# Four sigmoids and a tanh in place of exp, log1p and squared sums in a fused attention and feed-forward kernel

## The chip, the cores and the metric

The kernel runs on one core of a Trainium2 chip. The metric is the device time of one execution in microseconds (us). A core has engines that run side by side[...]: TensorE (PE in the profile, with PEld for its weight loads), VectorE (DVE), ScalarE (ACT), GpSimd (POOL) and SyncE (SP), which here only issues DMAs.

## The reference

Hashed attention comes first: queries and keys are hashed to six bits, and a query sees only the keys of its bucket. There are 4 x 8 heads of 768 x 64. Its output, as 3072 tokens of 512 values, goes through a feed-forward block:

```python
def _moe_ref(x, w_in, w_out) -> np.ndarray:   # x 3072x512, w_in 512x2048, w_out 2048x512
    h = x @ w_in
    sp = np.maximum(h, 0.0) + np.log1p(np.exp(-np.abs(h)))
    g = h * erf(sp)
    return (g @ w_out).astype(np.float32)
```

The activation is thus h times erf(log(1 + exp(h))). The change concerns only how erf(log(1 + exp(h))) is computed.

## The kernel before

The program has two stages. The attention stage takes some 320 us; it makes x and, beside its matmuls, brings the weights into SBUF. Its instructions are the same in both kernels. Then `feed_forward` runs, with everything in fp32.

`feed_forward` takes the tokens in 6 tiles of 512, and each tile in 4 chunks of the 2048 hidden values, so there are 24 chunks, numbered p. In each chunk both matrix products are done by a Strassen scheme of seven half-size products:

- `product` (L1204) makes P1 to P7, the parts of h, with four matmuls of 128x256 each. They go into one PSUM bank X, in the order P1, P6, P7, P4, P2, P5, P3, each after the bank has been emptied. `read` (L1222, ACT) copies a part from the bank into h in SBUF, `complete` (L1226, DVE) adds a later part to it. In the first three chunks, while the output banks are not in use, the products use those instead of X.
- The elementwise work runs on two units of a chunk, v = 0 and 1, of 128x1024 elements each: 48 units in all. A unit is ready when its four parts have been read and completed.
- `presum_g` (L1301, DVE) makes the sums of the activated h that Strassen's scheme wants, and `project` (L1344) makes M1 to M7 with four matmuls each, summed in PSUM over the four chunks of a tile. `combine` (L1359 on ACT, L1375 on DVE) puts the seven sums of a tile together and sends the output.

One unit passes through these steps before the change:

| step | engine, line | what it does |
|---|---|---|
| clip | DVE L1233 | e = min(h, 3.98) |
| exponential | ACT L1239 | e = exp(e) |
| one_more | ACT L1243 | w = 1 + e |
| lost | DVE L1248 | w = (w - 1) - e, the rounding lost in 1 + e |
| logarithm | ACT L1254 | e = log(1 + e) |
| correct | DVE L1258 | s = e - w |
| square | ACT L1262 | z = s squared |
| factor, 3 times | ACT L1267 | q = (z + c) squared, c from the tile cq |
| multiply, 3 times | DVE L1271 | s = (q + constant) * s |
| saturate | ACT L1282 | s = tanh(constant * s) |
| gate | DVE L1286 | h = h * s |

exp and log lie in different activation tables, so table loads (ACT_TABLE_LOAD) stand between them in ACT's queue.

The order of the instructions on every engine is fixed when the program is built, by `arrange` (L118). It is a list scheduler: each step is given as an `Op` with an engine, a cost, what it comes after, and a rank. The products and reads have ranks that begin with 0, the elementwise steps and `project` with 1 and then p plus a due time from `PRIORITY`. At each step the planner takes, on each engine, the ready step that can start first, and by rank where several can; it adds 1.28 where an ACT step changes the table. It also counts buffers:

```python
for each in arrange(ops, dict(h=8, e=4, w=6, wt=2), PATIENCE):
    each.emit()
```

There are eight tiles h (two per chunk), four tiles e, six tiles w, and two tiles wt for weight sums, which SP reloads from DRAM. The engines then work through their fixed orders, each waiting where its next instruction isn't ready.

Of the kernel before, what the change touches and what calls it, by code (L numbers as in the profile page):

```python
# [54 lines left out]
F32 = mybir.dt.float32  # L55
# [3 lines left out]
AF = mybir.ActivationFunctionType  # L59
ALU = mybir.AluOpType  # L60
# [3 lines left out]
P = 128  # L64
# [3 lines left out]
TINY = 3.242492675781250e-05  # L68
EPS = 2.0**-100
BOUND = 40.0  # L70
H_MAX = 3.98
ERF_LEAD = 1.418517747371711e-07
ERF_Q = (
    (6.2794604751645355, 19.35174303303216),
    (-5.316226701641483, 239.37499811839012),
    (-20.943483610527835, 66.98472325796595),
)


# [1 line left out]
class Op:  # L81
# [16 lines left out]


PRIORITY = dict(  # L100
    clip=(-0.37, 0.71),
    exponential=(3.56, 5.29),
    one_more=(4.45, -12.01),
    lost=(-10.26, -0.21),
    logarithm=(-0.61, 0.06),
    correct=(-8.09, -7.53),
    square=(-0.08, -1.35),
    factor=((-5.24, -2.71, -0.94), (-0.59, 2.14, 1.15)),
    multiply=((-3.33, 5.43, 8.37), (-6.26, 8.92, -4.28)),
    saturate=(-9.79, -1.73),  # L110
    gate=(9.64, -1.5),
    presum_g=(4.49, -4.94, 6.75, 0.67),
    project=-7.76,
)
# [79 lines left out]
def kernel(  # L194
# [11 lines left out]
    nc = tc.nc  # L206
# [16 lines left out]
    scale = 1.0 / D**0.5  # L223
    assert D == 64 and S == 768 and DM == JP * P and NT == B * S and NK == 4

    const = ctx.enter_context(tc.tile_pool(name="const", bufs=1))
# [10 lines left out]
    ones = const.tile([P, D], F32, name="ones")  # L237
    sgn = const.tile([P, 1], F32, name="sgn")
    tiny2 = const.tile([P, 1], F32, name="tiny2")
    cq = const.tile([P, len(ERF_Q)], F32, name="cq")  # L240
    w_in_sb = const.tile([P, NK, DFF], F32, name="w_in_sb")
    w_out_sb = const.tile([P, NF, DM], F32, name="w_out_sb")
    w_sum = const.tile([P, 3, 2, FH], F32, name="w_sum")
# [7 lines left out]
    for ab in range(2):  # L251
        rows = slice(ab * D, ab * D + D)
        nc.vector.tensor_copy(
            out=proj_sb[rows, ab * QR : ab * QR + NBIT],
            in_=proj_in[rows, ab * NBIT : (ab + 1) * NBIT],
# [4 lines left out]
    for c, (end, factor) in enumerate(  # L260
# [12 lines left out]
            out=steps[:, c : c + 1],  # L273
            in0=row,
            scalar1=float(end),
            scalar2=factor * BIG,
            op0=ALU.is_lt,
            op1=ALU.mult,
# [4 lines left out]
    for ab in range(2):  # L283
        rows = slice(ab * D, ab * D + D)
        nc.vector.tensor_copy(
            out=proj_q[rows, ab * QB : ab * QB + NBIT],
            in_=proj_in[rows, ab * NBIT : (ab + 1) * NBIT],
# [3 lines left out]
    nc.vector.tensor_copy(out=weight_q[D + QR : P, :], in_=weight_q[D : D + QR, :])  # L291
    nc.vector.memset(sgn, -(2.0**-27))
    nc.vector.memset(tiny2, TINY * TINY)
    for j, (c, _) in enumerate(ERF_Q):
        nc.vector.memset(cq[:, j : j + 1], c)

    def bank(name):
# [859 lines left out]
    def feed_forward(check, late):  # L1157
        again = late is None
        with (
# [11 lines left out]
            st = {}  # L1171

            def own(what):
                return work.tile([P, 2 * T], F32, name=what, tag=what, bufs=dict(e=4, w=6)[what])
# [53 lines left out]
            def unit(p, v):  # L1228
                return st[p]["h", v][:, :, :, :].rearrange("p f u t -> p (f u t)")

            def clip(p, v):
                e = st[p]["e", v] = own("e")
                nc.vector.tensor_scalar(  # L1233
                    out=e, in0=unit(p, v), scalar1=H_MAX, scalar2=None, op0=ALU.min
                )

            def exponential(p, v):
                e = st[p]["e", v]
                nc.scalar.activation(out=e, in_=e, func=AF.Exp)  # L1239

            def one_more(p, v):
                w = st[p]["w", v] = own("w")
                nc.scalar.activation(out=w, in_=st[p]["e", v], func=AF.Identity, bias=1.0)  # L1243

            def lost(p, v):

                w = st[p]["w", v]
                nc.vector.scalar_tensor_tensor(  # L1248
                    out=w, in0=w, scalar=-1.0, in1=st[p]["e", v], op0=ALU.add, op1=ALU.subtract
                )  # L1250

            def logarithm(p, v):
                e = st[p]["e", v]
                nc.scalar.activation(out=e, in_=e, func=AF.Ln, bias=1.0)  # L1254

            def correct(p, v):
                s = st[p]["s", v] = st[p].pop(("e", v))
                nc.vector.tensor_tensor(out=s, in0=s, in1=st[p].pop(("w", v)), op=ALU.subtract)  # L1258

            def square(p, v):  # L1260
                z = st[p]["z", v] = own("w")
                nc.scalar.activation(out=z, in_=st[p]["s", v], func=AF.Square)  # L1262

            def factor(p, v, j):
                z = st[p]["z", v]
                q = st[p]["q", v, j] = z if j == 2 else own("w")
                nc.scalar.activation(out=q, in_=z, func=AF.Square, bias=cq[:, j : j + 1])  # L1267

            def multiply(p, v, j):
                s = st[p]["s", v]  # L1270
                nc.vector.scalar_tensor_tensor(  # L1271
                    out=s,
                    in0=st[p].pop(("q", v, j)),
                    scalar=ERF_Q[j][1],
                    in1=s,
                    op0=ALU.add,
                    op1=ALU.mult,
                )

            def saturate(p, v):  # L1280
                s = st[p]["s", v]
                nc.scalar.activation(out=s, in_=s, func=AF.Tanh, scale=ERF_LEAD)  # L1282

            def gate(p, v):
                h = unit(p, v)
# [108 lines left out]
            def op(name, engine, cost, rank, fn, args, **more):  # L1394
                ops.append(Op(name, engine, cost, rank, lambda: fn(*args), **more))
# [70 lines left out]
            def between_ops(p, v):  # L1466
                me = (p, v)
                parts = tuple((what, p, q) for q in (v, v + 2) for what in ("read", "complete"))
                previous = None
                for k, (fn, engine, cost, after, more) in enumerate(  # L1470
                    (
                        (clip, "DVE", 0.69, parts, dict(take=("e", me))),
                        (exponential, "ACT", 1.05, (), dict(table="exp")),
                        (one_more, "ACT", 1.05, (), dict(take=("w", ("w", me)))),
                        (lost, "DVE", 1.22, (), {}),
                        (logarithm, "ACT", 1.05, (), dict(table="ln")),
                        (correct, "DVE", 1.22, (), dict(free=(("w", ("w", me)),))),
                        (square, "ACT", 1.05, (), dict(take=("w", ("z", me)))),
                    )
                ):  # L1480
                    after += (previous,) if previous else ()
                    if again and previous is None:
                        after += tuple(("gate", p - 1, n) for n in range(2))
                    previous = (fn.__name__, p, v)
                    rank = (1, p + PRIORITY[fn.__name__][v], 0)
                    op(previous, engine, cost, rank, fn, me, after=after, **more)
                squared = previous
                previous = ("correct", p, v)
                for j in range(len(ERF_Q)):
                    last = j == len(ERF_Q) - 1  # L1490
                    key = ("w", ("z" if last else j, me))
                    others = tuple(("factor", p, v, i) for i in range(j)) if last else ()
                    op(
                        ("factor", p, v, j),
                        "ACT",
                        1.14,
                        (1, p + PRIORITY["factor"][v][j], 0),
                        factor,
                        (p, v, j),
                        after=(squared,) + others,  # L1500
                        take=None if last else key,
                    )
                    op(
                        ("multiply", p, v, j),
                        "DVE",
                        1.22,
                        (1, p + PRIORITY["multiply"][v][j], 0),
                        multiply,
                        (p, v, j),
                        after=(("factor", p, v, j), previous),  # L1510
                        free=(key,),
                    )
                    previous = ("multiply", p, v, j)
                op(
                    ("saturate", p, v),
                    "ACT",
                    1.1,
                    (1, p + PRIORITY["saturate"][v], 0),
                    saturate,
                    me,  # L1520
                    after=(previous,),
                    table="exp",
                )
                op(
                    ("gate", p, v),
                    "DVE",
                    1.22,
                    (1, p + PRIORITY["gate"][v], 0),
                    gate,
                    me,  # L1530
                    after=(("saturate", p, v),),
                    free=(("e", me),),
                )
# [117 lines left out]
            for t in range(1, NTILE):  # L1651
                first, last = (t - 1) * NC4, t * NC4 - 1
# [133 lines left out]
```

## Time and profile before

| | us |
|---|---|
| time, median of 3 runs | 915.97 |
| lowest and highest run | 914.96, 917.1 |
| profiled execution: span | 913.2 |
| time of the profiled execution around its span | not given by the page |
| ACT_TABLE_LOAD in all | 51 of 1.283 |

The span goes from the first to the last instruction of one execution under the profiler. The times of the runs include what lies around the span. A busy share is the time in which an engine had an instruction in work; it doesn't say that the engine sets the time. "L1222" is line 1222 of the kernel, "h<-X" says that tile h is written from tile X, and a bracket such as "[0.68 <-ACT h L1222]" gives the idle time ahead of an instruction and what ended it. A matmul in fp32 appears as two records, so a product of four matmuls is shown as x8.

### The profile page before, as it was taken

To read this page: it belongs to the slowest core of one execution; us is meant where nothing else is said; L and a number is where in the kernel's file an instruction comes from. 1 tells how busy PE (TensorE), PEld (TensorE's weight loads), DVE (VectorE), ACT (ScalarE), POOL (GpSimd) and SP (SyncE) were. 2 spreads that over 40 slices of the span, in tenths; PEclk is the share of its full clock that TensorE was granted. 3 is DMA by queue.
4 is the path that set the end of the run, shared out by engine and by line. 5 is a ranking of instruction groups with operands and counts; after the bars stand their busy time and mean duration, and the time that the engine had idled before them with its cause. 6 is when DMAs were issued, how large, how long until landed. Compare 5 with 4: busy or idle time off the path is not lost.

```text
span 913.2 us, 13136 instructions
## 1 busy us (share of the span) xinstructions
PE 902.6 (99%) x5016; PEld 661.3 (72%) x5016; DVE 819.4 (90%) x1021; ACT 767.5 (84%) x1002; POOL 45.1 (5%) x80
## 2 busy tenths in 40 slices
PE   9999999999999999999999999999999999999997
PEld 5444444444444488888888888888888888888885
DVE  5999999999999979899999799998999889988995
ACT  6888887888877749999988998899989988899892
POOL 0211111111111000000000000000000000000000
PEclk9999999999999999999999999999999999999999
DMA  8455675655673131101021112211221121111211
GB/s 202 129 164 155 175 182 166 186 162 150 185 189 104 59 122 64 47 34 70 12 86 65 35 50 71 76 35 47 69 81 35 35 79 37 35 35 47 70 36 50
DMA packets 62854, 82.91 MB, mean 91 GB/s; under 512 B 34108, under 2 KB 47260, under 8 KB 62784
## 3 DMA queue, kind: packets, MB, share of 16 engines
q1 hardware_dynamic: 56384, 63.81, 24.5%
q0 software_dynamic: 5952, 17.72, 6.1%
q8 instruction: 41, 0.67, 0.3%
q10 hardware_dynamic: 448, 0.46, 0.2%
q14 instruction: 29, 0.24, 0.1%
HBM read 64.67 MB, written 17.30 MB: 90 GB/s over the span
## 4 chain that ended last, share of the span: by engine, by line
PE 91%; DVE 2%; issue 1%; DMA 1%; ACT 0%; POOL 0%; DVEq 0%; ACTq 0%; POOLq 0%
PE M L1344 31%; PE X L1204 28%; PE st L548 14%; PE av L629 12%; PE M L1204 3%; PE z_ps L664 1%; PE bits L817 1%; DMA raw<-in_w_in_dram 1%; DVE e L1258 0%; DVE h L1286 0%; DVE S L1301 0%; DVE h L1226 0%; DVE x_sum L340 0%; DVE w L1248 0%; ACT h L1222 0%
## 5 line engine op out<-in xcount | busy, mean ns | idle before, releaser
L1271 DVE SCALAR_TENSOR_TENSOR e<-w,e 128x1024 f32<-128x1024 f32 x144 | 173.3, 1219 | 5.8 <-ACT w L1267 3.0
L1267 ACT ACTIVATE w<-w,cq 128x1024 f32<-128x1024 f32 x144 | 160.6, 1143 | 1.9
L566 ACT ACTIVATE e_all<-st 128x768 f32<-128x768 f32 x192 | 150.8, 813 | 11.9 <-PE st L548 10.1
L548 PE MATMUL st<-q,k 64*128 64x384 f32 x768 | 155.0, 483 | 0.0
L1344 PE MATMUL M<-w_out_sb,h 128*128 128x256 f32 x576 | 140.2, 380 | 0.4 <-DVE h L1286 0.4
L629 PE MATMUL av<-e_all,v 128*64 128x385 f32 (+1 forms) x768 | 131.1, 490 | 0.0
L1204 PE MATMUL X<-x,w_in_sb 128*128 128x256 f32 x512 | 121.2, 380 | 0.0
L1344 PEld LDWEIGHTS M<-w_out_sb,h 128*128 128x128 f32 x576 | 109.4, 190 | 15.8 <-DVE h L1286 1.1
L1204 PEld LDWEIGHTS X<-x,w_in_sb 128*128 128x128 f32 x512 | 97.1, 190 | 13.7 <-ACT h L1222 0.6
L629 PEld LDWEIGHTS av<-e_all,v 128*64 128x64 f32 x768 | 52.4, 136 | 67.2 <-issue 64.5
L1344 PE MATMUL M<-wt,S 128*128 128x256 f32 x384 | 93.4, 379 | 0.4 <-DVE S L1301 0.4
L548 PEld LDWEIGHTS st<-q,k 64*128 64x128 f32 x768 | 68.2, 188 | 35.0 <-issue 34.4
L1204 PE MATMUL X<-x_sum,w_sum 128*128 128x256 f32 x344 | 81.7, 380 | 1.8 <-ACT h L1222 1.8
L1344 PEld LDWEIGHTS M<-wt,S 128*128 128x128 f32 x384 | 72.9, 190 | 10.6 <-DVE S L1301 0.8
L1204 PEld LDWEIGHTS X<-x_sum,w_sum 128*128 128x128 f32 x344 | 65.1, 190 | 11.9 <-ACT h L1222 3.3
L1222 ACT COPY h<-X 128x512 f32<-128x512 f32 x85 | 49.0, 576 | 22.3 <-PE X L1204 21.4
L1248 DVE SCALAR_TENSOR_TENSOR w<-w,e 128x1024 f32<-128x1024 f32 x48 | 58.4, 1220 | 9.7 <-ACT w L1243 9.6
L548 PE MATMUL st<-both 64*128 64x384 bf16 x384 | 62.9, 324 | 0.7 <-ACT e_all L566 0.4
L1286 DVE TENSOR_TENSOR h<-h,e 128x1024 f32<-128x1024 f32 x48 | 57.9, 1219 | 6.1 <-ACT e L1282 5.9
L1262 ACT ACTIVATE w<-e 128x1024 f32<-128x1024 f32 x48 | 50.4, 1050 | 13.2 <-DVE e L1258 13.0
L1258 DVE TENSOR_TENSOR e<-e,w 128x1024 f32<-128x1024 f32 x48 | 57.4, 1218 | 2.7 <-ACT e L1254 2.6
L1226 DVE TENSOR_TENSOR h<-X,h 128x512 f32<-128x512 f32 x65 | 44.8, 689 | 16.4 <-PE X L1204 15.4
(131 smaller groups left out, 1377.3 us busy)
## 6 DMA issues: line engine op xcount, KB each, us to landing
wt<-wt SPq DMA_DIRECT2D x24, 768.0 KB, 4.1
raw<-in_w_out_dram POOLq DMA_DIRECT2D x16, 512.0 KB, 4.4
raw<-in_w_in_dram POOLq DMA_DIRECT2D x14, 512.0 KB, 4.3
v<-in_v_dram SPq DMA_DIRECT2D x32, 192.0 KB, 4.7
xs<-x SPq DMA_DIRECT2D x16, 384.0 KB, 2.4
q<-in_qkT_dram SPq DMA_DIRECT2D x30, 192.0 KB, 4.1
k<-in_qkT_dram SPq DMA_DIRECT2D x30, 192.0 KB, 4.5
r<-rd SPq DMA_DIRECT2D x30, 192.0 KB, 3.4
```

Source lines behind the costliest of these rows:

```text
L548: nc.tensor.matmul(out=st[:, ab, 0:HS], lhsT=d["k" + src][rows, keys], rhs=d["q" + src][rows, cols], start=(part == 0), stop=(part == 1),)
L566: nc.scalar.activation(out=e[:, :, 0:HS], in_=st[:, :, 0:HS], func=AF.Exp, scale=scale)
L629: nc.tensor.matmul(out=d["av"][rows, 0:w], lhsT=d["v"][:, g * GC + c, rows], rhs=e[:, ab, 0:w], start=(g == 0 and c == 0), stop=(g == 1 an ...
L1204: nc.tensor.matmul(out=d[where][:, u, :], lhsT=a[:, kc, f : f + P], rhs=b[:, kc, :], start=(first and u == 0 and kc == 0), stop=(last and ...
L1222: nc.scalar.copy(out=quarter(p, q), in_=st[p][where])
L1248: nc.vector.scalar_tensor_tensor(out=w, in0=w, scalar=-1.0, in1=st[p]["e", v], op0=ALU.add, op1=ALU.subtract)
L1258: nc.vector.tensor_tensor(out=s, in0=s, in1=st[p].pop(("w", v)), op=ALU.subtract)
L1262: nc.scalar.activation(out=z, in_=st[p]["s", v], func=AF.Square)
L1267: nc.scalar.activation(out=q, in_=z, func=AF.Square, bias=cq[:, j : j + 1])
L1271: nc.vector.scalar_tensor_tensor(out=s, in0=st[p].pop(("q", v, j)), scalar=ERF_Q[j][1], in1=s, op0=ALU.add, op1=ALU.mult,)
L1286: nc.vector.tensor_tensor(out=h, in0=h, in1=st[p].pop(("s", v)), op=ALU.mult)
L1344: nc.tensor.matmul(out=banks[name][:, sub, :], lhsT=a[:, u, sub * P : (sub + 1) * P], rhs=b[:, u, :], start=(c == 0 and k == 0), stop=(c = ...
```

## The change

The seven steps from clip to square go. In their place, four sigmoids are taken directly of h, and their product, each but the first with a constant added, goes into the tanh:

| step | engine | what it does |
|---|---|---|
| lead | ACT | s = sigmoid(h + bias) |
| factor, 3 times | ACT | q = sigmoid(a * h + b), b from the tile cq |
| multiply, 3 times | DVE | s = (q + constant) * s |
| saturate | ACT | s = tanh(constant * s) |
| gate | DVE | h = h * s |

All four sigmoids read h and can start as soon as the unit is ready; every factor takes a tile w, and lead takes the tile e. Lead, factor and saturate are given to the planner as one table, "sigmoid". The due times of these steps are nearly all alike, where before each step had its own.

```diff
+GATE_LEAD = float(np.exp(0.024672653620378578))
+GATE_BIAS = 0.2070990400060388
+GATE_S = tuple(
+    (a, b, float(np.exp(d)))
+    for a, b, d in (
+        (1.0042202890675247, -2.7392697200635756, -1.6980318627393862),
+        (0.9963684715182539, -0.22837759957137604, 0.7457328010609228),
+        (1.6743181256578874, -5.977511012430903, 0.8413097454356667),
+    )
 )
...
 PRIORITY = dict(
-    clip=(-0.37, 0.71),
-    exponential=(3.56, 5.29),
-    one_more=(4.45, -12.01),
-    lost=(-10.26, -0.21),
-    logarithm=(-0.61, 0.06),
-    correct=(-8.09, -7.53),
-    square=(-0.08, -1.35),
-    factor=((-5.24, -2.71, -0.94), (-0.59, 2.14, 1.15)),
-    multiply=((-3.33, 5.43, 8.37), (-6.26, 8.92, -4.28)),
-    saturate=(-9.79, -1.73),
-    gate=(9.64, -1.5),
+    lead=(-0.6, -0.6),
+    factor=((-0.6, -0.6, -0.6), (-0.6, -0.6, -0.6)),
+    multiply=((-0.5, -0.5, -0.5), (-0.5, -0.5, -0.5)),
+    saturate=(-0.5, -0.5),
+    gate=(-0.4, -0.4),
...
+            def lead(p, v):
+                s = st[p]["s", v] = own("e")
+                n = len(GATE_S)
+                nc.scalar.activation(out=s, in_=unit(p, v), func=AF.Sigmoid, bias=cq[:, n : n + 1])
 
             def factor(p, v, j):
-                z = st[p]["z", v]
-                q = st[p]["q", v, j] = z if j == 2 else own("w")
-                nc.scalar.activation(out=q, in_=z, func=AF.Square, bias=cq[:, j : j + 1])
+                q = st[p]["q", v, j] = own("w")
+                nc.scalar.activation(
+                    out=q, in_=unit(p, v), func=AF.Sigmoid, scale=GATE_S[j][0], bias=cq[:, j : j + 1]
+                )
...
             def saturate(p, v):
                 s = st[p]["s", v]
-                nc.scalar.activation(out=s, in_=s, func=AF.Tanh, scale=ERF_LEAD)
+                nc.scalar.activation(out=s, in_=s, func=AF.Tanh, scale=GATE_LEAD)
...
+                op(
+                    ("lead", p, v),
+                    "ACT",
+                    1.14,
+                    (1, p + PRIORITY["lead"][v], 0),
+                    lead,
+                    me,
+                    after=parts,
+                    take=("e", me),
+                    table="sigmoid",
+                )
+                previous = ("lead", p, v)
+                for j in range(len(GATE_S)):
+                    key = ("w", (j, me))
                     op(
                         ("factor", p, v, j),
                         "ACT",
                         1.14,
-                        (1, p + PRIORITY["factor"][v][j], 0),
+                        (1, p + PRIORITY["factor"][v][j], 1 + j),
                         factor,
                         (p, v, j),
-                        after=(squared,) + others,
-                        take=None if last else key,
+                        after=parts,
+                        take=key,
+                        table="sigmoid",
                     )
```

More of the change, by code (lines that the diff above doesn't have):

```diff
@@ L70 @@
 BOUND = 40.0
[L71 to L76, printed above, removed]
+GATE_LEAD = float(np.exp(0.024672653620378578))
[7 more added lines that the diff above has]
+    )
 )
@@ L239 @@
     tiny2 = const.tile([P, 1], F32, name="tiny2")
-    cq = const.tile([P, len(ERF_Q)], F32, name="cq")
+    cq = const.tile([P, len(GATE_S) + 1], F32, name="cq")
     w_in_sb = const.tile([P, NK, DFF], F32, name="w_in_sb")
@@ L293 @@
     nc.vector.memset(tiny2, TINY * TINY)
-    for j, (c, _) in enumerate(ERF_Q):
+    for j, c in enumerate([b for _, b, _ in GATE_S] + [GATE_BIAS]):
         nc.vector.memset(cq[:, j : j + 1], c)
@@ L1229, in unit, with factor @@
                 return st[p]["h", v][:, :, :, :].rearrange("p f u t -> p (f u t)")
[L1231 to L1234, printed above, removed]
-                )
[L1237 to L1264, printed above, removed]
-                z = st[p]["z", v]
-                q = st[p]["q", v, j] = z if j == 2 else own("w")
-                nc.scalar.activation(out=q, in_=z, func=AF.Square, bias=cq[:, j : j + 1])
+            def lead(p, v):
+                s = st[p]["s", v] = own("e")
+                n = len(GATE_S)
+                nc.scalar.activation(out=s, in_=unit(p, v), func=AF.Sigmoid, bias=cq[:, n : n + 1])
+            def factor(p, v, j):
+                q = st[p]["q", v, j] = own("w")
+                nc.scalar.activation(
+                    out=q, in_=unit(p, v), func=AF.Sigmoid, scale=GATE_S[j][0], bias=cq[:, j : j + 1]
+                )
             def multiply(p, v, j):
@@ L1273, in multiply @@
                     in0=st[p].pop(("q", v, j)),
-                    scalar=ERF_Q[j][1],
+                    scalar=GATE_S[j][2],
                     in1=s,
@@ L1468, in between_ops @@
                 parts = tuple((what, p, q) for q in (v, v + 2) for what in ("read", "complete"))
[L1469 to L1492, printed above, removed]
+                if again:
+                    parts += tuple(("gate", p - 1, n) for n in range(2))
+                op(
[12 more added lines that the diff above has]
+                    key = ("w", (j, me))
                     op(
@@ L1521, in between_ops @@
                     after=(previous,),
-                    table="exp",
+                    table="sigmoid",
                 )
```

## The prediction

> **What bounds the kernel now.** I read the page's busy shares first, then its 40 slices, then busy time by stretches, then TensorE's timeline. Busy shares and slices:
>
> ```profile
> PE 902.6 (99%) x5016; PEld 661.3 (72%) x5016; DVE 819.4 (90%) x1021; ACT 767.5 (84%) x1002; POOL 45.1 (5%) x80
> ...
> PE   9999999999999999999999999999999999999997
> PEld 5444444444444488888888888888888888888885
> DVE  5999999999999979899999799998999889988995
> ACT  6888887888877749999988998899989988899892
> ```
>
> Three engines look full. PEld jumps from 4 to 8 at slice 15: attention ends there and the feed-forward stage begins. Stretches of that stage (columns: us, then busy us of PE, PEld, DVE, ACT, POOL with instructions, clock, DMA share, GB/s):
>
> ```profile
> 345.00:400.00 55.00, 54.33 (x251) 47.28 (x250) 51.54 (x58) 53.63 (x58) 0.00 (x0) 1.00 0.14 46
> 400.00:450.00 50.00, 48.97 (x226) 42.39 (x225) 47.23 (x54) 47.76 (x51) 0.00 (x0) 1.00 0.14 53
> ...
> 600.00:650.00 50.00, 50.00 (x234) 44.05 (x233) 43.86 (x50) 45.65 (x48) 0.00 (x0) 1.00 0.11 38
> ...
> 850.00:907.00 57.00, 56.46 (x260) 48.70 (x258) 50.97 (x56) 42.12 (x42) 0.00 (x0) 1.00 0.11 38
> ```
>
> From 500 to 850 us PE has no idle time, at full clock, while ACT and DVE are busy some 90%. A busy PE need not be a PE at its peak, so I take the distance between starts. In TensorE's timeline one Strassen product (4 matmuls, 8 records) starts 1.727 us after the one before (347.82, 349.55, 351.28, 353.00): 0.4316 us per matmul, with nothing lost between. The stage has 24 chunks x 7 products x 4 = 672 matmuls for h and 672 for the output: 1,344 x 0.4316 = 580.1 us. With the divisors (327.84 to 328.30) and the bound (340.58 to 340.79) it is 580.8. The stage runs from 320.73 to 906.7 (last start 904.98 plus 8 x 0.2158): 586.0. **So PE can lose at most 5.2 us in this stage.** The starts in TensorE's timeline show where:
>
> ```profile
> 358.18 1.89 PE L1204 MATMUL X<-x,w_in_sb 128*128 128x256 f32 x8
> 360.75 1.99 PE L1204 MATMUL X<-x_sum,w_sum 128*128 128x256 f32 x8 [0.68 <-ACT h L1222]
> ...
> 434.40 1.99 PE L1204 MATMUL X<-x_sum,w_sum 128*128 128x256 f32 x8 [0.68 <-ACT h L1222]
> 436.75 0.70 PE L1344 MATMUL M<-w_out_sb,h 128*128 128x256 f32 x2 [0.35 <-DVE h L1286]
> ```
>
> 358.18 + 1.727 = 359.91, so the product at 360.75 is 0.84 late, and it runs 0.1 longer after the wait: 0.94. By the same sum: 0.19 at 385, 0.83 at 434, 0.73 at 437, 0.67 at 484, 0.26 at 755, and 0.89 in the last chunk (893.8, 897.4, 899.7, waits for a gate or a presum). Together **4.5 us**; the other 0.7 lies at the small matmuls of attention, which stay. After 906.7 come 6.5 us of the last sums and output DMAs.
>
> **What the Trainium skill says.** Trace Analysis, "Identifying the Most-Contended Engine", calls matmul busy share a poor measure and asks for LDWEIGHTS busy share. The trace agrees: at no idle PEld shows 44.05 of 50 us, 88%, which is 190 ns of every 215.8, while in attention PE shows 99% at about half that PEld. ScalarE: Activation LUTs, "What ACT_TABLE_LOAD costs", gives 1283 ns for a load plus about 1380 of drain; the trace has 1283, and no drain: the load at 337.44 follows an activation that ends at 337.43. The same section says that every function costs the same and a per-partition bias adds about 93 ns: L1267 with a bias tile takes 1143, L1262 without 1050. "Table sets: the hidden batching unit" puts tanh into the sigmoid set; no run here shows that yet, but the built order of the changed kernel has one table load ahead of its first sigmoid and none after it in this pass.
>
> **The change part by part.** Groups of before that go:
>
> ```profile
> L1248 DVE SCALAR_TENSOR_TENSOR w<-w,e 128x1024 f32<-128x1024 f32 x48 | 58.4, 1220 | 9.7 <-ACT w L1243 9.6
> L1258 DVE TENSOR_TENSOR e<-e,w 128x1024 f32<-128x1024 f32 x48 | 57.4, 1218 | 2.7 <-ACT e L1254 2.6
> L1239 ACT ACTIVATE e<-e 128x1024 f32<-128x1024 f32 x48 | 50.3, 1053 | 7.7 <-DVE e L1233 7.6
> L1254 ACT ACT_TABLE_LOAD x25 | 32.1, 1283 | 0.4
> ```
>
> *ACT.* Gone per unit: exp, add one, log, square: 50.3 + 50.6 + 49.3 + 50.4 = 200.6 us. Gone: 50 table loads (25 + 16 + 9) = 64.1. New: 48 leads with a bias tile, 48 x 1.143 = 54.9, and one load, 1.3. The 144 factors (Square to Sigmoid, same shape and bias tile) and 48 tanh stay at 160.6 and 49.8. Net -208.5: 767.5 becomes 559.0.
>
> *DVE.* Gone: clip 32.2, lost 58.4, correct 57.4 = 148.0. The 144 multiplies (same instruction, other constants) and 48 gates stay. 819.4 becomes 671.4; one more memset (about 0.1) lies in the start-up.
>
> *What of this is on the path.* Almost nothing: ACT and DVE leave the stage with 305 and 379 us of work beside PE's 581 (513.4 - 208.5 and 526.6 - 148.0, the page's sums less those to 320.8). The cover of the removed work is PE's own stream, which keeps every instruction. What can be won is the 4.5 us of waits.
>
> *Order.* PE's order changes too, since the planner gets other costs and due times. Counting output matmuls M between consecutive products in the built order: before, the runs ahead of the waits at 360.75, 434.40 and 437.29 are 0, 0 and 1. After, from the 23rd product on every run is 3 to 11. A product that follows another in bank X must wait for that bank to be emptied: 359.91 to 360.75 shows 0.84 us for it with ACT free, 0.95 with a complete on DVE (0.689 in place of 0.576). Three M's are 1.295, so 0.34 us of slack remain. The runs of 8 and 11 stand ahead of the second product of a chunk: there a read waits on ACT behind eight activations issued in one burst (8 x 1.143 = 9.1 us), or for a buffer h that the M's themselves free.
>
> *The added waits.* A lead and its factors wait for four quarters of h, and behind them on ACT stand the reads that free X for PE. Planned costs are near the trace: 1.14 against 1.143, tanh 1.1 against 1.052, 1.22 against 1.219, read 0.58 against 0.576, so the plan should hold. The start is tightest. The first M, after 18 products (21 before), is due at 351.28 + 1.73 = 353.0. By hand from the built order: last quarter of the first unit at 332.8, lead to 333.9 (335.2 if its table load waits with it), three more reads, two leads of the next chunk and six factors to about 348.9, two tanh to 351.0, the gates 350.5 to 352.9. That is 0 to 0.3 late; if load and reads shift everything, 2.4. The tail: 90 M's (38.8 us) follow the last product, 83 before; ACT's remaining burst is 8 x 1.143 + 2 x 1.05 = 11.3 us, DVE's about 10, so the waits of 0.89 go. If any wait is late next, it is a read behind a burst.
>
> *SP, POOL.* Both queues keep their counts; weight tiles land in 4.1 us with two buffers against 24 us per chunk. Nothing.
>
> **Sum.** 4.5 us go, I leave 0.8 for the start and scattered waits (bounds 0 and 4.5): -3.7. Span 913.2 becomes 909.5. The page states no time of that execution beyond its span; the median of the runs, 915.97, lies 2.8 above it, and I keep that: **912.3**. The 0.2% that a measurement can tell is 1.8 us.
>
> **Rivals.**
> - *The waits only move (0.16).* For: the due times put all activations of a chunk in one burst, which before were strewn among the reads. Against: every run is 3 or more. Half to all of the 4.5 us come back in other places: 914.2 to 917.6, about 915.5.
> - *The read behind the burst stops PE in every chunk (0.07).* Place: ahead of P6 of each chunk after the third, 21 times; M's ahead of it cost 0.43 each, so the plan is no finer than that. Slower beyond the noise from (4.5 + 1.8) / 21 = 0.30 us a chunk; at 0.43 it is +9.0 - 4.5: 920.5. Against: the planned ACT costs are not below the trace's, and factors in a row start only 1.11 apart (three took 3.37).
> - *ACT and DVE set the end now, so a large part of 208 us is won.* For: both are near 90% full. Against: 580.8 of 586.0 is issue time of matmuls that all stay. It would need a PE below 0.4316 per matmul: no chance given.
> - *It doesn't do what it says*, tanh taking a table of its own: one load in the built order excludes it.
>
> **Numbers.** Likeliest case 0.77: 912.3, by itself 911.2 to 914.1. Faster 0.77, within 0.16, slower 0.07. The range leaves out most of the slower case and the end of the second: 910.9 to 916.4.
>
> **What would show it.** Right: PE still 99%, PEld 88% through the whole stage, the last matmul ending near 903, ACT near 559 and DVE near 671, one load. The start is right if the first M stands at 353 without a wait over 0.3. Wrong: waits of PE for L1222 ahead of P6 in each chunk; starts of products no longer 1.727 apart; or an end below 901.5 (320.73 + 580.8), for which the sum has no room.

## The result and the profile after

The changed kernel takes 912.87 us (median of 5 runs, 911.35 to 913.09) against 915.97 (5 runs too): a ratio of 0.9962, 95% interval 0.9949 to 0.9974, or 3.5 us less by the ratio, 2.4 to 4.7 by its interval. 912.3 was predicted. The profiled execution's span is 910.5 us, 2.7 below the one before.

The page after, in the same rows as before:

```profile
PE 900.9 (99%) x5016; PEld 662.0 (73%) x5016; DVE 682.0 (75%) x878; ACT 564.8 (62%) x809; POOL 45.3 (5%) x80
...
PE   9999999999999999999999999999999999999996
PEld 5444444444444478888888888888888888888885
DVE  4989999999898969986566557656776557656652
ACT  6878887888887849755545554555555545545420
```

In the feed-forward stage ACT's busy time falls from 513 to 311 us and DVE's from 526 to 389, and PE's row looks as it did. The difference for PE is visible only in the stretches (us, then busy us of PE, PEld, DVE, ACT, POOL, clock, DMA share, GB/s):

```profile
345.00:400.00 55.00, 55.00 (x257) 48.40 (x256) 51.12 (x57) 40.66 (x46) 0.00 (x0) 1.00 0.17 60
400.00:450.00 50.00, 50.00 (x234) 44.01 (x233) 31.41 (x36) 28.43 (x32) 0.00 (x0) 1.00 0.11 38
...
600.00:650.00 50.00, 50.00 (x233) 44.03 (x232) 29.55 (x34) 27.00 (x31) 0.00 (x0) 1.00 0.14 47
```

The two stretches that lacked 0.67 and 1.03 us of PE are full now, and PEld stands at 88% in them too. TensorE's timeline at the place of the first long wait of before:

```profile
354.13 0.59 PE L1317 MATMUL M<-w_out_sb,h 128*128 128x256 f32 x2
354.56 1.89 PE L1204 MATMUL M<-x,w_in_sb 128*128 128x256 f32 x8
...
359.74 1.89 PE L1204 MATMUL X<-x,w_in_sb 128*128 128x256 f32 x8
361.47 1.89 PE L1317 MATMUL M<-w_out_sb,h 128*128 128x256 f32 x8
363.19 1.89 PE L1204 MATMUL X<-x_sum,w_sum 128*128 128x256 f32 x8
```

The product that came 0.84 us late now has four output matmuls (x8 records) ahead of it, and every eight records start 1.72 or 1.73 after the eight before. Going through all starts of the stage, none is over 0.15 us late. Its first and last lines, of before and then of after:

```profile
320.73 3.72 PE L1204 MATMUL M<-x,w_in_sb 128*128 128x256 f32 x16
904.98 1.89 PE L1344 MATMUL M<-w_out_sb,S 128*128 128x256 f32 x8
```

```profile
321.88 3.72 PE L1204 MATMUL M<-x,w_in_sb 128*128 128x256 f32 x16
901.48 1.89 PE L1317 MATMUL M<-w_out_sb,S 128*128 128x256 f32 x8
```

The stage runs from 321.88 to 903.21 (last start 901.48 plus 8 x 0.2158): **581.3 us, where it was 586.0**. Its matmuls alone were put at 580.8.

So 4.6 us went in the stage (585.97 less 581.33 before rounding), and the profiled spans differ by 2.7. The rest lies outside it: the stage began 1.15 us later (321.88 against 320.73) and what follows the last matmul took 7.3 us against 6.5. The experiments show how far these two vary.

### The profile page after: what moved, and what is told of

It is laid out like the page before. It is cut to its first block, busy times and chain, and to the rows that moved or that the text cites. A ratio compares the mean times of both kernels' runs of the same rounds, so it can differ in the third digit from the quotient of the medians.

```text
span 910.5 us, 12823 instructions
## 1 busy us (share of the span) xinstructions
PE 900.9 (99%) x5016; PEld 662.0 (73%) x5016; DVE 682.0 (75%) x878; ACT 564.8 (62%) x809; POOL 45.3 (5%) x80
## 4 chain that ended last, share of the span: by engine, by line
PE 92%; issue 1%; DMA 1%; ACT 0%; POOL 0%; DVE 0%; DVEq 0%; ACTq 0%; POOLq 0%
PE M L1317 32%; PE X L1204 28%; PE st L548 14%; PE av L629 12%; PE M L1204 3%; PE z_ps L664 1%; PE bits L817 1%; DMA raw<-in_w_in_dram 0%; POOL both L855 0%; ACT e_all L566 0%; ACT keep L468 0%; DMA bd<-sg 0%; DVE u L1348 0%; ACT x L688 0%; DVEq L1695 0%
## 5 line engine op out<-in xcount | busy, mean ns | idle before, releaser
L1238 ACT ACTIVATE w<-h,cq 128x1024 f32<-128x1024 f32 x144 | 155.3, 1135 | 0.0
L1234 ACT ACTIVATE e<-h,cq 128x1024 f32<-128x1024 f32 x48 | 55.1, 1149 | 109.7 <-DVE h L1226 109.6
L1317 PE MATMUL M<-wt,S 128*128 128x256 f32 x384 | 95.4, 379 | 0.0
L1255 ACT ACTIVATE e<-e 128x1024 f32<-128x1024 f32 x48 | 50.4, 1054 | 29.9 <-DVE e L1244 29.9
L548 PEld LDWEIGHTS <-both 64*128 64x128 bf16 x384 | 19.6, 94 | 43.1 <-issue 21.5
```

The lines of the kernel that those rows point to most:

```text
L548: nc.tensor.matmul(out=st[:, ab, 0:HS], lhsT=d["k" + src][rows, keys], rhs=d["q" + src][rows, cols], start=(part == 0), stop=(part == 1),)
L1234: nc.scalar.activation(out=s, in_=unit(p, v), func=AF.Sigmoid, bias=cq[:, n : n + 1])
L1238: nc.scalar.activation(out=q, in_=unit(p, v), func=AF.Sigmoid, scale=GATE_S[j][0], bias=cq[:, j : j + 1])
L1255: nc.scalar.activation(out=s, in_=s, func=AF.Tanh, scale=GATE_LEAD)
L1317: nc.tensor.matmul(out=banks[name][:, sub, :], lhsT=a[:, u, sub * P : (sub + 1) * P], rhs=b[:, u, :], start=(c == 0 and k == 0), stop=(c = ...
```

## The experiments

The theory: TensorE's own stream sets the length of the stage, and the 4.5 us of waits were built into the order of the kernel before, which the planner could not avoid with ACT and DVE so full. The rivals: the table loads themselves made the waits; the even due times took them away; ACT or DVE, or a chain over both, still sets the end. Twelve runs were made; each has its own median and its ratio to the kernel before on the same chip. The end of the stage is taken throughout as the last start plus its records at 0.2158 us.

**The changed kernel once more** (no edit).

> The changed kernel once more, for the spread of its stages between executions. Theory (TensorE's own stream sets the stage, and the waits of before are gone): time 912.9 within 1; feed-forward stage 581.3 us from its first product to the end of its last matmul, no wait of TensorE over 0.2 in it. If the later start of the stage (321.88 against 320.73) and the longer end (7.3 against 6.5 us) come from the change, they stand here again to 0.2; if they are chance of one execution, they differ here.

Measured: 911.63 us, ratio 0.9961 (0.9946 to 0.9975). The time is 0.3 below the stated band. Stage 581.33 again, no wait. It starts at 321.90 and 7.46 us follow it, so both stand again to 0.2, which was to mean that they come from the change. That test is weak, for the same start comes about in different ways: against the kernel before, TensorE in the first profile falls back by 0.35 us before 7 us and by 0.80 at 63, in the second by 0.65 at 63 and by 0.52 at 180. Over the nine profiles of this study without a wait of over 1 us, the two compared included, the stage begins between 320.73 and 322.06, and what follows it takes 6.4 to 7.7 us.

The spans of all executions are on record and tell more. If the stage is as long in each as in the profiled one of its kernel, an estimate, 327.8 us lie outside it on average in 41 executions of the kernel before (those measured beside the runs of this section), and 329.1 in ten of the changed kernel. So some 1.3 us are lost outside the stage with the change. It isn't a matter of chance alone, and its cause is open: five executions with more work on ACT, further down, have 327.1.

**One matmul in 56 less.**

```diff
                     for f in range(4):
+                        if name == "M7" and f == 1:
+                            continue
```

> The changed kernel without one of the four matmuls of M7 in each chunk (24 of 1,344; their part of the output is left out). Theory (TensorE's stream sets the stage): 24 x 0.4316 = 10.4 us less, 902.5 within 1. Rival (a chain over ACT and DVE is as long as TensorE's stream by now): 5 us less or fewer.

Measured: 901.33 us, ratio 0.9848 (0.9831 to 0.9864). The stage is 570.97 us, 10.36 less than 581.33, which is 24 x 0.4316 = 10.36. The time is 0.2 below the stated band; the stage is exact. Each matmul counts in full: TensorE's stream is the stage.

**Less elementwise work.**

```diff
 GATE_S = tuple(
...
-)
+)[:1]
```

> The changed kernel without two of the three factors and their multiplies (left out of the product). ACT loses 96 x 1.14 = 109 us, DVE 96 x 1.22 = 117. Theory: nothing of it is on the path, 912.9 within 1, stage 581.3. Rival (ACT and DVE still set the end, or the tail hangs on the last chunk's chain): 3 us or more faster, 910 or less.

Measured: 911.61 us beside 911.63 for the changed kernel, measured together; stage 581.33. DVE went from 682.0 to 568.5 and ACT from 564.8 to 467.2, for nothing. Both times lie 0.3 below the band, which was set from the first measurement of the changed kernel. That excludes a chain over ACT and DVE as the limit, in the middle and in the tail.

**The table loads taken from the kernel before.**

```diff
-                nc.scalar.activation(out=e, in_=e, func=AF.Ln, bias=1.0)
+                nc.scalar.activation(out=e, in_=e, func=AF.Tanh, bias=1.0)
```

> The kernel before with Tanh in place of Ln and nothing else (the activation's value is another): the order of all instructions is that of before, and the 50 table loads of the feed-forward stage are gone (64 us of ACT). Theory (the order has 0 and 1 output matmuls ahead of the products at 360.75, 434.40 and 437.29, and those waits are built in): the 0.94 at 360.75 and most of the 0.8 at 434 stay, those elsewhere (385, 484, 755, the last chunk) go: 1.5 to 2.5 of the 4.5 us gone, time 913.5 to 914.5. Rival (table loads make all the waits): 912.5 or less. Rival (they make none): 916.

Measured: 915.58 us, ratio 1.0003 (0.9994 to 1.0012). ACT's busy time fell from 767.5 to 702.7, and the stage is 585.59 (585.98 before). The expectation, that the waits at 385, 484 and 755 and in the last chunk would go, was wrong: only the two smallest went, 0.19 us each at 385 and 893.8, and the others stayed within 0.03. TensorE's timeline of this kernel:

```profile
361.20 2.00 PE L1204 MATMUL X<-x_sum,w_sum 128*128 128x256 f32 x8 [0.67 <-ACT h L1222]
...
434.66 2.00 PE L1204 MATMUL X<-x_sum,w_sum 128*128 128x256 f32 x8 [0.67 <-ACT h L1222]
437.01 0.70 PE L1344 MATMUL M<-w_out_sb,h 128*128 128x256 f32 x2 [0.35 <-DVE h L1286]
...
899.76 2.00 PE L1344 MATMUL M<-wt,S 128*128 128x256 f32 x8 [0.43 <-DVE S L1301]
```

The brackets are those of before (0.68, 0.68, 0.35, and 0.41 at 899.69). With 65 us less on ACT and the same order, these waits are the same, so they do not come from a full ACT. The two for a read stand where a product follows another directly in bank X: the order puts nothing between. The waits for a gate and a sum end on DVE, whose load this run leaves as it was (819.0 us busy), so for those two it doesn't tell the order from a full DVE.

**The table loads given back to the changed kernel.**

```diff
-                nc.scalar.activation(out=s, in_=s, func=AF.Tanh, scale=GATE_LEAD)
+                nc.scalar.activation(out=s, in_=s, func=AF.Exp, scale=GATE_LEAD)
...
                 op(
                     ("saturate", p, v),
...
-                    table="sigmoid",
+                    table="exp",
```

Here, and in the kernel with even sums and more on DVE below, an output matmul also looks up the weight sums only if they have been made.

> The changed kernel with Exp in place of the last Tanh, given to the planner as another table: 47 more table loads in the built order, with the number of all other instructions kept (the gate's value is another). Theory: 47 x 1.283 = 60 us more on ACT, which then has 365 of 581 us in the stage, are hidden; the built order has one run of 0 output matmuls, which costs about 0.9: time 913 to 914.5. Rival (the table loads were what made the kernel before slow): 2.5 to 4 us come back, 915.5 to 917.

Measured: 911.94 us beside 911.63, measured together. In the groups of this kernel (line, engine, operation, count, busy us, mean ns, idle time before):

```profile
L1255 ACT ACT_TABLE_LOAD x24 | 30.8, 1283 | 0.4
L1234 ACT ACT_TABLE_LOAD x22 | 28.2, 1283 | 61.0 <-DVE h L1226 60.9
```

With two more at L1238, 48 loads take 61.6 us of ACT, and the stage is 582.85 us: 1.5 longer, with one product 0.84 late where the order has no output matmul ahead, and one 0.51 late. The stage was expected 0.9 longer. The time stayed 1.1 below the band, which was set from 912.9. Sixty us of table loads cost 1.5 us of the stage, and nothing that shows in the time, when ACT has room.

**The due times of before in the changed kernel.**

```diff
-    lead=(-0.6, -0.6),
-    factor=((-0.6, -0.6, -0.6), (-0.6, -0.6, -0.6)),
-    multiply=((-0.5, -0.5, -0.5), (-0.5, -0.5, -0.5)),
-    saturate=(-0.5, -0.5),
-    gate=(-0.4, -0.4),
+    lead=(-0.37, 0.71),
+    factor=((-5.24, -2.71, -0.94), (-0.59, 2.14, 1.15)),
+    multiply=((-3.33, 5.43, 8.37), (-6.26, 8.92, -4.28)),
+    saturate=(-9.79, -1.73),
+    gate=(9.64, -1.5),
```

> The changed kernel with the due times of before for lead (those of clip), factor, multiply, saturate and gate. Theory: with this much room on ACT and DVE the due times don't matter; no run of output matmuls below 3 in the built order, stage 581.3 to 582, time 912.9 within 1. Rival (the even due times are what took the waits away): 2 to 4 us of waits come back, 915 to 917.

Measured: 912.21 us, ratio 0.9962 (0.9949 to 0.9974), stage 581.51, no start over 0.15 late. The even due times are not what took the waits away.

**The even due times in the kernel before** (clip to square and factor -0.6, multiply and saturate -0.5, gate -0.4).

> The kernel before with the even due times of the changed kernel (-0.6, multiplies and saturate -0.5, gate -0.4) and its own steps. The built order has 0 output matmuls ahead of eight products, 1 ahead of three. Theory (at 90% on ACT and DVE the order matters): 8 x 0.9 + 3 x 0.4 = 8.4 us of waits and some in the tail, in place of 4.5: time 919.5 to 922. Rival (even due times are as good): 916.

Measured: 971.92 us, ratio 1.0617 (1.0598 to 1.0636): 56 us slower, where 4 to 7 were expected. The direction was right and the count of output matmuls between products misses the main cost. TensorE's waits in this kernel (engine, line, waited for: us, times, longest):

```profile
PE M L1344 <- DVE h L1301: 40.3, 4, 10.9
```

L1301 is `presum_g`. Its third sum, which M7 needs, keeps the due time 6.75, while a multiply is now due at -0.5. When DVE always has a multiply ready, those of later chunks pass the sum, and M7 waits for it about 10 us, four times. This account is tested below.

**More work on ACT, on DVE, on both.** In the changed kernel, copies on ACT (1.0 us each in the plan) and additions of zero on DVE (1.22) were set between lead and the first multiply, one after the other: A four times, D three times, and A D A D A D A.

```diff
+            def extra_act(p, v, k):
+                s = st[p]["s", v]
+                nc.scalar.copy(out=s, in_=s)
+
+            def extra_dve(p, v, k):
+                s = st[p]["s", v]
+                nc.vector.scalar_tensor_tensor(
+                    out=s, in0=s, scalar=0.0, in1=s, op0=ALU.mult, op1=ALU.add
+                )
```

> The changed kernel with four more ACT copies of a unit between lead and the first multiply (about 48 x 4 x 1.0 = 192 us): ACT back to some 500 of 581 us in the stage, as full as before, DVE left at 379. The built order has two products with no output matmul ahead of them (23rd and 31st). Theory (it takes both engines full, since a unit goes to and fro between them): waits of 1.8 to 2.5 us at these two places and in the start, none later: time 914.5 to 915.5. Rival (a full ACT alone brings the waits of before back): 4.5 us or more, 917 and up. Rival (waits came from DVE alone): 912.9.

> The changed kernel with three more DVE operations of a unit (144 x 1.22 = 176 us): DVE at some 555 of 581 us in the stage, fuller than before, ACT left at 305. The built order has 0 output matmuls ahead of four products and 1 ahead of three. Theory: 0.9 for each 0 and 0.4 for each 1, together 4 to 5.5 us: time 916.5 to 918.5; the places are those of the built order. Rival (ACT alone makes the waits): 912.9. Rival (TensorE hides it all): 912.9.

> The changed kernel with four more ACT copies and three more DVE operations of a unit, one after the other: ACT at some 500 and DVE at 555 of 581 us in the stage, with one table and even due times. The built order has 0 ahead of seven products. Theory (how full both engines are makes the waits): 7 x 0.9 and some more in the start and the tail, 6 to 9 us, time 918.5 to 922, slower than before, whose due times fit its chain better. Rival (one table makes the difference): the same as the changed kernel, 912.9.

Measured: with ACT 912.24 us, ratio 0.9963 (0.9949 to 0.9977); with DVE 1027.24, ratio 1.1214 (1.1195 to 1.1232); with both 968.81, ratio 1.0585 (1.0567 to 1.0603).

ACT alone: its busy time is 749.7 us, nearly that of before, and the stage is 583.35, 2.0 longer than in the changed kernel, with two products 0.84 late, as expected for the stage; the time is 2.3 below the band and doesn't show even these 2.0. So a full ACT is hidden but for 2.0 us. DVE was the surprise, by 110 us, and both together by 47. TensorE's waits with DVE alone, and one of them in DVE's and TensorE's timelines:

```profile
PE M L1327 <- DVE h L1284: 63.1, 5, 14.3
PE M L1327 <- DVE S L1284: 30.0, 1, 30.0
```

```profile
538.77 1.89 PE L1204 MATMUL X<-x,w_in_sb 128*128 128x256 f32 x8
554.75 3.38 PE L1327 MATMUL M<-w_out_sb,h 128*128 128x256 f32 x8 [14.08 <-DVE h L1284]
```

```profile
540.74 3.74 DVE L1242 SCALAR_TENSOR_TENSOR e<-e 128x1024 f32<-128x1024 f32 x3
544.39 5.95 DVE L1254 SCALAR_TENSOR_TENSOR e<-w,e 128x1024 f32<-128x1024 f32 x5
550.26 2.43 DVE L1269 TENSOR_TENSOR h<-h,e 128x1024 f32<-128x1024 f32 x2
552.61 0.68 DVE L1284 TENSOR_TENSOR S<-h 128x512 f32<-128x512 f32 x1
```

While PE stands still from 540 to 554.75, DVE does three additions, five multiplies and two gates ahead of sums. It isn't short of time as a whole (554 us busy of the 705 from 320 to 1025); its order is bad. The two engines together (968.81) give fewer such waits than DVE alone, so the load alone does not tell how bad the order becomes.

**The sums made due with the gates**, in the kernel with more on DVE and in the kernel before with even due times.

```diff
-    presum_g=(4.49, -4.94, 6.75, 0.67),
+    presum_g=(-0.4, -0.4, -0.4, -0.4),
```

> The kernel with three more DVE operations per unit, now with presum_g due with the gate (-0.4 four times) in place of 4.49, -4.94, 6.75 and 0.67. There TensorE waited five times 6 to 14 us, and once 30, for a sum that stood on DVE behind multiplies of later chunks. Theory (the even due times let multiplies pass the sums, which shows only when DVE has no room): these waits go; what stays are the products without output matmuls ahead (4 to 5 of 0.9) and one early wait of 0 to 25 us for weight sums, which the planner ranks last of all: time 917 to 942. Rival (555 us of DVE beside 581 us of TensorE can't be hidden in any order): over 1000.

> The kernel before with even due times, now with presum_g even too (-0.4 four times). Theory: the four waits of about 10 us for the third sum go, and with them most of the 56 us: time 916 to 930. Rival (the steps of before need their own due times whatever the sums do): 950 and up.

Measured: 951.18 us (ratio 1.0386, 1.0368 to 1.0403), in place of 1027.24; and 946.14 (1.0333, 1.0316 to 1.0350), in place of 971.92. Both miss their bands, 917 to 942 and 916 to 930. The first bears the theory out all the same: the five waits for a sum are gone, and the one early wait is 30 us long where 0 to 25 was allowed. Its stretches for PE (us, busy us with instructions, clock, DMA share, GB/s) and the wait:

```profile
420.00:470.00 50.00, 16.68 (x61) 0.69 0.08 32
470.00:520.00 50.00, 50.00 (x234) 1.00 0.25 84
...
820.00:870.00 50.00, 50.00 (x233) 1.00 0.11 38
```

```profile
460.72 3.78 PE L1327 MATMUL M<-wt,h 128*128 128x256 f32 x8 [30.21 <-DVE wt L1299]
```

Once the weight sums (ranked last by the planner) are made, PE runs without idle time from 470 to 920 us, although DVE is as busy as in the bad order: 841.1 and 845.9 us in all, and from 520 on 45.5 to 47.1 of every 50 us. A nearly full DVE can be hidden, in the right order. In the second kernel 26 of the 56 us went. The waits for the third sum are gone; what is left are waits of 0.2 to 1.5 us for gates, completes and reads throughout, and 9.8 and 3.1 for gates in the last chunks:

```profile
PE M L1344 <- DVE h L1286: 16.6, 9, 9.8
```

So the steps of before need due times of their own besides those of the sums; which ones wasn't found.

## Why the prediction was right

- *What bounds the kernel.* Right. 580.8 us was put as the matmuls' own time, 581.3 was measured, and taking 24 matmuls away took 10.36 us.
- *What can be won.* 4.5 us of waits were counted, 4.6 went in the stage. No rival of the prediction came about: the waits did not move, and no read behind a burst stopped PE.
- *The start.* The first M was due at 353.0, with 0 to 0.3 late by hand. It stands at 354.13 in a stage that began 1.15 later, so at 352.98, without a wait. The two gates run from 351.55 to 353.90; less 1.15 that is 350.4 to 352.75, against 350.5 to 352.9 by hand. ACT's timeline shows why the table load did no harm: it runs in an idle time ahead of the lead.

```profile
330.41 1.28 ACT L1234 ACT_TABLE_LOAD   x1
333.93 1.15 ACT L1234 ACTIVATE e<-h,cq 128x1024 f32<-128x1024 f32 x1 [2.24 <-DVE h L1226]
```

- *What was mis-sized.* 0.8 us was left for the start and scattered waits: there were none. The lengths outside the stage were taken as fixed. They vary by over 1 us from execution to execution, and are about 1.3 us longer on average in the changed kernel. So the stage gained 0.9 more than was forecast and the rest lost more than that. That the two nearly cancel, and the time comes out within 0.6 of the forecast, is luck; that the gain is small, and where it arises, is not. The 2.8 us that were added to the span isn't a fixed length either: in every execution of the two kernels with a span on record the time lies 1.7 to 1.9 above it. The other 1.0 is that the profiled execution of before was a short one.
- *Busy times.* DVE was put at 671.4 and is 682.0, ACT at 559.0 and is 564.8. Busy time is a union: back to back, instructions of 0.69 us start 0.61 apart (899.67 and 900.28 in DVE's timeline before), and this overlap goes where idle time opens between them. What was taken off was too much by that. Nothing in the sum hung on it, nor on the 21 products that the prediction counts ahead of the first M before, where the trace has 23.
- *The argument from the order.* For this kernel it held: no product in X without three output matmuls ahead of it after the 22nd, no wait. As a count it was too weak: in the kernels with a full DVE it missed waits of 6 to 30 us ahead of output matmuls, for sums.
- *One table.* The changed kernel's trace has one load in the stage, at L1234, for its sigmoids and tanh together. The prediction gave this no worth of its own, and that nearly holds: 50 loads taken from the kernel before gained 0.4 us of the stage, 48 given back cost 1.5, and neither shows in the time. With ACT filled up again (the run with more on ACT) 2.0 of the 4.6 us came back. That leaves 2.6 that room on ACT doesn't explain, so the freed room on DVE has a part in giving the planner an order without waits. No run took DVE's share alone out of the kernel before, so this last step is argued.

## What to carry to other kernels

When one engine is saturated, the work of the others is worth only the waits that it causes: here 203 us of ACT and 137 us of DVE, measured as busy time, were worth under 5. Count those waits from the distances between starts on the saturated engine, and ask of each whether an instruction comes late or whether the fixed order left nothing to do; the second kind did not answer to a faster helper until the order was made anew. And even due times, which did no harm while the helper engines had room, came with a kernel 6% slower in the steps of before and 12% slower with a full DVE. So a planner's ranks should be tried under load and not only where they are used.

## What the runs showed of the hardware

After a long wait TensorE is slow for a while: the eight records after the 14 us wait took 3.38 us and those after the 30 us wait 3.78, where eight take 1.89, and the granted clock was 0.69 in the stretch of 50 us that holds the longest wait. After idle times of 0.68 us the next product was only 0.1 longer (1.99 where others take 1.89). A table load cost ACT 1.30 us in all, by an estimate: without 50 of them its busy time fell by 64.8.
